# Gated linear attention and a hard-swish feed-forward block on one core: stores on another queue, idle products, and a new order

One core of a Trainium2 chip. The metric is the device time of one execution in microseconds (us), the median of several runs.

## The reference, cut to what matters

```python
# q, k, v: 4 x 8 x 768 x 48, alpha the same shape in 0.8 .. 1.0, all float32
for t in range(S):
    state = alpha[:, :, t, :, None] * state + einsum('bhd,bhe->bhde', k[:, :, t], v[:, :, t])
    y[:, :, t] = einsum('bhd,bhde->bhe', q[:, :, t], state)
x = y.transpose(0, 2, 1, 3).reshape(3072, 384)
h = x @ w_in                      # w_in 384 x 2048, float64 in memory
g = h * clip(h + 3, 0, 6) / 6
out = g @ w_out                   # w_out 2048 x 384, float64 in memory
```

## The kernel before

The sequence is cut into 24 chunks of 128 steps (index j), two chunks make a group g of 256 tokens, 12 groups in all. The kernel is one list of small steps. A step is a function that emits a few instructions; the list fixes the order on each engine. Groups 0 and 1 use plain products (`f`, `b`), while the 64-bit weights come in and are converted; the later groups use a fast matrix multiplication with fewer products (`M` for w_in, `P` for w_out).

What the argument touches:

```python
    bank_m = [ps.tile([C, GT * 2], FP, tag=f"m{i}", name=f"m{i}_ps") for i in range(4)]

    def store2(g, i):                         # 44 output stores of 96 KB
        row, col = PLACES[i]
        j = G * g + row
        nc.sync.dma_start(out=out[j * C : (j + 1) * C, col * HD : (col + 1) * HD],
                          in_=oh_t.pop((g, i)))
    # ... store(c): two more of 192 KB, also nc.sync; all loads are nc.sync too

    with tc.manual_schedule():
        run("""lk.0 la.0 lq.0 la.1 tk.0 lq.1 ta.0 ca.0 lv.1 tq.0 r.0 w.1 ta.1 ca.1 p.0 tq.1 r.1 q.0
            la.2 k.0 p.1 sc.0 lk.1 lv.0 q.1 d1.1 kb.0 m.0 w.0 d2.1 ta.2 ck.0 d3.1 tk.1 ca.2 u.0
            ...""")
```

In the list: `la lk lq lv` load chunk j, `w` loads a slice of weights and `d1`..`d4` convert it; `ta tk tq` bring alpha, k, q into the layout of the scans (`r`, `p`, on the vector engine, DVE) and `k`, `q` scale by them; `sc m kb ck u yi yx cy` are the attention products on the tensor engine (PE) with their evictions, and `cy` hands x to the first feed-forward product `f` (line L417 before, L420 after). `P` is L621 before and L630 after, `M` is L521 and L530, the outputs of DVE are L637 and L646. The scalar engine is ACT.

Of the kernel before, what the change touches and what calls it, by code (L numbers as in the profile page):

```python
# [16 lines left out]
def kernel(  # L17
# [35 lines left out]
    C = 128  # L53
# [195 lines left out]
    def load_v(j):  # L249
        to = ring["v", j % NV].rearrange("s (p a) e -> s p a e", a=2)  # L250
        sv = rows(v, j).rearrange("(p a) s d -> s p a d", a=2)
        nc.sync.dma_start(out=to[:, :, 0, 0:D], in_=sv[:, :, 0])
        nc.sync.dma_start(out=to[:, :, 1, 64 - D : 64], in_=sv[:, :, 1])
# [99 lines left out]
    def update(j):  # L353
        if last(j):
            return
        u = bank("u", j).rearrange("r p n -> r (p n)")[:, 0 : NP * 2 * D].rearrange(
            "r (p n) -> r p n", p=NP)
        ps_t["u", j] = u
        vs = ring["v", j % NV]
        for p in range(NP):  # L360

            one = vs[:, 2 * p]
            both = bass.AP(one.tensor, one.offset, [one.ap[0], (C - D, 2), (1, D)])
            nc.tensor.matmul(u[:, p], kb_t[j][:, p], both, start=True, stop=True)  # L364
# [16 lines left out]
    def within(j):  # L381
        y, A, vs = bank("y", j), A_t[j], ring["v", j % NV]
# [17 lines left out]
    def keep_x(j):  # L400
        g = j // G
        if j % G == 0:
            xT_t[g] = wk.tile([C, KT, GT], FP, tag="xT", name="xT")
# [48 lines left out]
    def store(c):  # L452
        nc.sync.dma_start(out=out[c * C : (c + 1) * C, :], in_=os_t.pop(c))
# [185 lines left out]
    def store2(g, i):  # L639
        row, col = PLACES[i]  # L640
        j = G * g + row
        nc.sync.dma_start(out=out[j * C : (j + 1) * C, col * HD : (col + 1) * HD],
                          in_=oh_t.pop((g, i)))
# [14 lines left out]
        "O": store2,  # L658
# [7 lines left out]
    with tc.manual_schedule():  # L666
        run("""lk.0 la.0 lq.0 la.1 tk.0 lq.1 ta.0 ca.0 lv.1 tq.0 r.0 w.1 ta.1 ca.1 p.0 tq.1 r.1 q.0
            la.2 k.0 p.1 sc.0 lk.1 lv.0 q.1 d1.1 kb.0 m.0 w.0 d2.1 ta.2 ck.0 d3.1 tk.1 ca.2 u.0
            k.1 d4.1 sm.0 w.4 sc.1 r.2 kb.1 ck.1 m.1 st.1 d1.0 u.1 p.2 d2.0 w.3 yi.0 d3.0 yi.1
            cy.0 yx.1 d1.4 sm.1 d4.0 d2.4 w.2 cy.1 f.0.1.0 d3.4 d1.3 st.2 d2.3 f.0.0.1 d4.4 la.3  # L670
            fr.0.1 fg.0.1 lk.2 d3.3 f.0.4.2 lv.2 fr.0.0 d1.2 lq.2 fg.0.0 d2.2 d4.3 w.5 tk.2
            fr.0.4 ta.3 d3.2 f.0.3.3 ca.3 r.3 lk.3 tq.2 fr.0.3 k.2 d4.2 w.6 q.2 fg.0.4 sc.2 d1.5
            p.3 d2.5 f.0.2.0 fg.0.3 d3.5 lq.3 tk.3 w.7 fr.0.2 kb.2 m.2 d4.5 ck.2 d1.6 k.3 u.2
            fg.0.2 d2.6 tq.3 sm.2 f.0.5.1 q.3 st.3 lv.4 d3.6 lk.5 sc.3 lv.3 fr.0.5 d1.7 fg.0.5
            la.4 yi.2 d4.6 m.3 d2.7 kb.3 w.8 yx.2 ck.3 d3.7 f.0.6.2 cy.2 d4.7 tk.5 w.9 fr.0.6
            yi.3 fg.0.6 f.0.7.3 d1.8 d2.8 lk.4 yx.3 d3.8 fr.0.7 ta.4 lq.4 cy.3 u.3 ca.4 lq.5
            d1.9 f.1.3.0 r.4 w.10 d2.9 fg.0.7 d4.8 sm.3 f.1.0.1 d3.9 fr.1.3 w.11 fg.1.3 st.4
            f.1.2.2 fr.1.0 p.4 d1.10 fg.1.0 d4.9 d2.10 tk.4 tq.4 fr.1.2 k.4 w.12 f.1.7.3 d3.10
            d1.11 fg.1.2 tq.5 d4.10 d2.11 f.1.4.0 q.4 fr.1.7 d3.11 w.13 f.1.1.1 fr.1.4 fg.1.7
            d4.11 d1.12 fg.1.4 d2.12 w.14 f.1.6.2 d3.12 fr.1.1 fg.1.1 d1.13 d4.12 b.0.0.3 d2.13  # L680
            fr.1.6 w.15 d3.13 sc.4 d1.14 fg.1.6 f.1.5.0 d4.13 m.4 d2.14 lv.5 d3.14 la.5 kb.4
            fr.1.5 yi.4 ck.4 la.6 fg.1.5 d1.15 d4.14 b.0.1 d2.15 d3.15 u.4 yx.4 sm.4 d4.15 b.0.2
            cy.4 y.1 y.5 y.6 ta.5 P.1.1.1 y.2 ca.5 x.0 r.5 b.1.0.2 y.3 p.5 b.0.3 k.5 st.5 q.5
            y.7 y.4 y.8 sc.5 bo.0 y.9 so.0 b.1.1 y.10 lq.6 m.5 y.11 la.7 y.15 yi.5 y.13 b.1.2
            y.16 y.0 tq.6 y.17 yx.5 y.12 y.19 b.1.3 cy.5 y.18 xc.2.1 y.20 xc.2.3 y.21 M.2.15.0
            xc.2.4 bo.1 s.1.0.0 P.1.0.3 s.1.1.1 x.1 s.1.4 M.2.16 K.1.0 s.1.2.2 P.1.3.2 s.1.3.3
            x.2 G.1.0 K.1.2 P.1.2 x.3 xc.2.5 y.23 M.2.0.1 xc.2.6 s.1.5 K.1.1 P.1.4 xc.2.0 xc.2.8
            xc.2.7 xc.2.2 xc.2.9 xc.2.10 y.14 ca.6 P.1.5 G.1.1 r.6 O.1.1 lq.7 y.22 P.1.6 p.6
            so.1 O.1.0 y.24 G.1.2 ca.7 M.2.7.2 n.2.0.8 tq.7 G.1.3 M.2.1 O.1.3 n.2.7.9 r.7 lk.6
            M.2.8 n.2.1.10 M.2.18.3 o.2.4.0 q.6 lk.7 e.2.4 M.2.2 p.7 n.2.18.11 M.2.17 n.2.2.12  # L690
            h.2.4 lv.6 M.2.19 tk.6 O.1.2 M.2.3 lv.7 q.7 k.6 M.2.4 la.8 tk.7 sc.6 n.2.4.13
            o.2.6.0 o.2.0.0 M.2.5 lq.8 k.7 e.2.0 M.2.9 m.6 n.2.5.14 sc.7 la.9 h.2.0 M.2.6.1
            o.2.1.0 m.7 e.2.1 M.2.10 h.2.1 kb.6 n.2.10.15 yi.6 ca.8 ck.6 M.2.11 o.2.5.0 cy.6
            tq.8 e.2.5 u.6 n.2.11.9 h.2.5 kb.7 sm.6 M.2.12 ck.7 o.2.7.0 yi.7 r.8 n.2.12.13
            M.2.13 o.2.3.0 u.7 o.2.7.1 st.7 n.2.13.12 o.2.3.1 e.2.7 M.2.14 o.2.2.0 e.2.3 yx.7
            h.2.7 h.2.3 P.2.0.3 cy.7 o.2.2.1 s.2.1.15 e.2.2 o.2.6.1 h.2.2 e.2.6 M.3.15.0
            s.2.3.11 K.2.0 h.2.6 P.2.1.1 sm.7 s.2.0.13 xc.3.1 s.2.4 M.3.16 s.2.2.12 P.2.3.2
            G.2.0 st.8 ca.9 xc.3.3 s.2.5 P.2.2 xc.3.4 K.2.2 xc.3.0 xc.3.5 r.9 xc.3.6 xc.3.7
            M.3.0.1 xc.3.8 xc.3.2 K.2.1 xc.3.9 p.8 P.2.4 n.3.0.9 xc.3.10 q.8 p.9 M.3.1 G.2.1
            O.2.1 P.2.6 n.3.1.14 lq.9 O.2.0 M.3.2 G.2.3 O.2.3 M.3.7.3 lk.8 n.3.2.10 P.2.5 tq.9  # L700
            n.3.7.8 o.3.4.0 lk.9 q.9 e.3.4 M.3.3 h.3.4 lv.8 G.2.2 M.3.8 tk.8 O.2.2 M.3.18.2 lv.9
            k.8 M.3.4 tk.9 la.10 n.3.18.13 sc.8 o.3.6.0 n.3.4.15 k.9 M.3.19 lq.10 o.3.0.0 m.8
            M.3.17 e.3.0 M.3.9 la.11 h.3.0 ca.10 sc.9 o.3.1.0 M.3.5 r.10 e.3.1 M.3.10 n.3.5.11
            h.3.1 kb.8 n.3.10.12 m.9 M.3.6.1 ck.8 M.3.11 o.3.5.0 p.10 e.3.5 u.8 n.3.11.8 yi.8
            h.3.5 sm.8 M.3.12 o.3.7.0 ca.11 st.9 yx.8 n.3.12.15 kb.9 o.3.7.1 cy.8 M.3.13 o.3.3.0
            ck.9 e.3.7 tq.10 yi.9 n.3.13.10 h.3.7 u.9 o.3.2.0 M.3.14 o.3.3.1 o.3.2.1 e.3.3 yx.9
            s.3.1.12 e.3.2 P.3.0.2 h.3.3 cy.9 h.3.2 s.3.3.13 o.3.6.1 sm.9 P.3.1.0 e.3.6 xc.4.1
            K.3.0 xc.4.0 h.3.6 xc.4.3 s.3.0.15 xc.4.4 M.4.15.1 s.3.4 P.3.3.3 s.3.2.8 G.3.0 st.10
            xc.4.5 s.3.5 P.3.2 K.3.2 xc.4.6 xc.4.7 xc.4.8 r.11 xc.4.2 M.4.0.0 xc.4.9 K.3.1
            xc.4.10 q.10 P.3.4 n.4.0.10 p.11 M.4.1 G.3.1 O.3.1 P.3.6 lq.11 n.4.1.11 O.3.0 M.4.16  # L710
            G.3.3 O.3.3 M.4.2 lk.10 M.4.7.2 tq.11 n.4.2.14 P.3.5 q.11 lk.11 n.4.7.9 o.4.4.0
            e.4.4 lv.10 h.4.4 M.4.3 tk.10 M.4.8 G.3.2 k.10 O.3.2 M.4.18.3 tk.11 lv.11 M.4.4
            n.4.18.12 la.12 k.11 sc.10 o.4.6.0 n.4.4.15 o.4.0.0 M.4.19 lq.12 m.10 e.4.0 M.4.9
            h.4.0 M.4.17 o.4.1.0 la.13 sc.11 ca.12 e.4.1 h.4.1 M.4.10 m.11 M.4.5 n.4.10.8 r.12
            kb.10 n.4.5.13 M.4.11 ck.10 o.4.5.0 M.4.6.0 n.4.11.9 p.12 e.4.5 u.10 o.4.7.0 M.4.12
            h.4.5 sm.10 yi.10 n.4.12.15 o.4.7.1 st.11 M.4.13 ca.13 e.4.7 yx.10 h.4.7 n.4.13.14
            yi.11 o.4.3.0 cy.10 o.4.2.0 M.4.14 o.4.3.1 o.4.2.1 yx.11 e.4.3 s.4.1.12 e.4.2
            P.4.0.3 h.4.3 cy.11 h.4.2 s.4.3.8 o.4.6.1 P.4.1.1 tq.12 e.4.6 K.4.0 h.4.6 xc.5.1
            s.4.0.9 xc.5.3 M.5.15.0 s.4.4 P.4.3.2 s.4.2.15 G.4.0 xc.5.4 s.4.5 xc.5.5 P.4.2
            xc.5.0 K.4.2 xc.5.6 xc.5.7 xc.5.8 r.13 xc.5.2 xc.5.9 M.5.0.1 xc.5.10 K.4.1 q.12  # L720
            P.4.4 p.13 n.5.0.14 M.5.1 G.4.1 O.4.1 P.4.6 lq.13 n.5.1.13 O.4.0 M.5.16 G.4.3 O.4.3
            M.5.2 lk.12 M.5.7.3 tq.13 n.5.2.11 P.4.5 q.13 lk.13 n.5.7.10 o.5.4.0 e.5.4 lv.12
            h.5.4 M.5.3 tk.12 M.5.8 G.4.2 k.12 O.4.2 M.5.18.2 tk.13 lv.13 M.5.4 n.5.18.9 la.14
            k.13 sc.12 o.5.6.0 n.5.4.12 o.5.0.0 M.5.19 lq.14 m.12 e.5.0 M.5.9 h.5.0 M.5.17
            o.5.1.0 la.15 sc.13 ca.14 e.5.1 h.5.1 M.5.10 m.13 M.5.5 n.5.10.8 r.14 kb.12 n.5.5.15
            M.5.11 ck.12 o.5.5.0 M.5.6.1 n.5.11.10 p.14 e.5.5 u.12 o.5.7.0 M.5.12 h.5.5 sm.12
            yi.12 n.5.12.12 o.5.7.1 st.13 M.5.13 ca.15 cy.12 e.5.7 kb.13 o.5.3.0 n.5.13.11 yi.13
            h.5.7 ck.13 o.5.2.0 M.5.14 o.5.3.1 yx.13 o.5.2.1 e.5.3 u.13 s.5.1.9 e.5.2 h.5.3
# [100 lines left out]
```

## Time and profile before

| | before |
|---|---|
| time, the 44 runs timed beside the experiments (four sets of 11, medians 585.8 to 586.4) | 584.1 to 590.2 us |
| the profiled run that the prediction read | 590.0 us (span 588.2) |
| PE busy in it | 97 % of the span |

To compare kernels I use one derived measure, **lost time**: at any matmul, the time since the start of the trace minus the sum of unit times of all useful matmuls issued before it. The unit times are those of the prediction (540.5 us for the whole kernel); idle products count as nothing. Reading the lost time at 30 us of useful work (the end of the head, about 50 to 55 us on the clock), at 200, and at the end tells in which stretch a kernel loses.

### The profile page before, as it was taken

The numbers are of one execution on the slowest core, as the hardware profiler recorded it, in microseconds if no ns is written. First come the engines' busy times: TensorE is split into PE (matmuls) and PEld (weight loads), VectorE is DVE, ScalarE is ACT, GpSimd is POOL, SyncE is SP. The second block draws the span as 40 slices with busy tenths as digits, with TensorE's granted clock in tenths as the row PEclk, the third lists the DMA queues.
The fourth block names the chain that finished last, engine by engine and source line by source line (L and its number), as shares of the span: only waits on it lengthen the run. The fifth ranks groups of instructions, "written<-read, shape, count | busy, mean of one in ns | idle before, by whom it ended". The sixth has DMA issues, their size and how long they took to land.

```text
span 588.2 us, 12191 instructions
## 1 busy us (share of the span) xinstructions
PE 568.7 (97%) x5032; PEld 527.9 (90%) x5032; DVE 474.4 (81%) x787; ACT 196.6 (33%) x335; POOL 49.7 (8%) x70
## 2 busy tenths in 40 slices
PE   5888999999999999999999999999999999999997
PEld 3777887689999899999999999999999999999997
DVE  7788698999996995995995995896897798685570
ACT  2454473012422332432331341341351251342520
POOL 2332233100000010000010010000000000000000
PEclk9598999999999999999999999999999999999999
DMA  9999754203503503503502601701700610500000
GB/s 159 212 183 195 194 158 109 64 1 104 112 1 85 119 1 77 127 3 79 123 2 53 151 1 38 161 8 34 163 7 14 161 30 1 128 1 1 2 28 27
DMA packets 87607, 45.82 MB, mean 78 GB/s; under 512 B 48896, under 2 KB 82432, under 8 KB 87552
## 3 DMA queue, kind: packets, MB, share of 16 engines
q1 hardware_dynamic: 87552, 45.05, 34.8%
q8 instruction: 39, 0.64, 0.5%
q14 instruction: 16, 0.13, 0.1%
HBM read 40.30 MB, written 4.72 MB: 77 GB/s over the span
## 4 chain that ended last, share of the span: by engine, by line
PE 71%; DVE 14%; DMA 6%; SPq 5%; issue 2%; ACT 1%; DVEq 0%; ACTq 0%
PE m_ps L621 27%; PE m_ps L521 20%; PE m_ps L417 7%; PE m_ps L443 4%; PE y_ps L386 3%; PE sc_ps L322 3%; PE u_ps L364 3%; SPq L246 2%; PE y_ps L396 2%; DMA kq<-in_k_dram 2%; DVE g_sb L425 2%; DVE g_sb L458 2%; DMA rings<-in_q_dram 2%; DVE k L268 1%; PE kb_ps L339 1%
## 5 line engine op out<-in xcount | busy, mean ns | idle before, releaser
L621 PE MATMUL m_ps<-w,g_sb 128*128 128x192 f32 x704 | 121.4, 328 | 0.2
L621 PEld LDWEIGHTS m_ps<-w,g_sb 128*128 128x128 f32 x704 | 113.7, 190 | 2.1 <-issue 0.8
L527 ACT COPY g_sb<-m_ps 128x512 f32<-128x512 f32 x110 | 64.2, 584 | 112.2 <-PE m_ps L521 110.8
L621 PE MATMUL m_ps<-rings,g_sb 128*128 128x192 f32 x528 | 91.7, 327 | 1.4 <-DVE oh L637 1.3
L521 PE MATMUL m_ps<-xc,w 128*128 128x128 f32 x640 | 86.1, 279 | 2.4 <-DVE oh L637 1.8
L621 PEld LDWEIGHTS m_ps<-rings,g_sb 128*128 128x128 f32 x528 | 85.6, 190 | 2.3 <-DVE oh L637 2.0
L521 PEld LDWEIGHTS m_ps<-xc,w 128*128 128x128 f32 x640 | 78.1, 192 | 5.4 <-DVE oh L637 2.7
L421 ACT ACTIVATE r<-g_sb,half 128x512 f32<-128x512 f32 x80 | 57.0, 721 | 75.0 <-DVE g_sb L462 34.3
L425 DVE SCALAR_TENSOR_TENSOR g_sb<-r,g_sb 128x512 f32<-128x512 f32 x80 | 54.8, 693 | 13.5 <-ACT r L421 12.1
L349 POOL TENSOR_TENSOR t<-t,R 128x384 f32<-128x384 f32 x20 | 20.0, 999 | 411.5 <-DVE t L376 229.6
L521 PE MATMUL m_ps<-xT,raw 128*128 128x128 f32 x400 | 51.6, 275 | 0.0
L521 PEld LDWEIGHTS m_ps<-xT,raw 128*128 128x128 f32 x400 | 49.4, 192 | 0.3
L268 DVE STREAM_TRANSPOSE q<-qq 128x512 f32<-128x512 f32 x18 | 20.2, 1121 | 36.5 <-DMA qq<-in_q_dram 36.5
L417 PE MATMUL m_ps<-xT,w 128*128 128x256 f32 x192 | 45.3, 392 | 1.1 <-ACT xT L404 1.1
L521 PE MATMUL m_ps<-xT,w 128*128 128x128 f32 x320 | 43.4, 279 | 0.1
L417 PEld LDWEIGHTS m_ps<-xT,w 128*128 128x128 f32 x192 | 36.9, 196 | 6.9 <-ACT xT L404 1.3
L568 DVE TENSOR_TENSOR g_sb<-g_sb 128x512 f32<-128x512 f32 (+1 forms) x55 | 41.6, 791 | 0.1
L521 PEld LDWEIGHTS m_ps<-xT,w 128*128 128x128 f32 x320 | 38.8, 192 | 1.7 <-ACT g_sb L527 0.3
L291 DVE TENSOR_TENSOR_SCAN R<-t,ones 128x516 f32<-128x516 f32 x24 | 30.1, 1252 | 4.4 <-ACT t L282 4.4
L521 PE MATMUL m_ps<-xc,raw 128*128 128x128 f32 x240 | 32.6, 279 | 0.0
L322 PE MATMUL sc_ps<-q,k 48*128 48x128 f32 x384 | 28.9, 291 | 3.5 <-DVE k L314 2.3
L521 PEld LDWEIGHTS m_ps<-xc,raw 128*128 128x128 f32 x240 | 29.7, 191 | 1.8 <-issue 1.6
(98 smaller groups left out, 711.2 us busy)
## 6 DMA issues: line engine op xcount, KB each, us to landing
raw<-in_moe_w_out_dram SPq DMA_DIRECT2D x8, 768.0 KB, 4.7
t<-in_v_dram SPq DMA_DIRECT2D x48, 96.0 KB, 2.8
raw<-in_moe_w_in_dram SPq DMA_DIRECT2D x24, 192.0 KB, 7.2
out_dram<-oh SPq DMA_DIRECT2D x44, 96.0 KB, 1.7
aq<-in_alpha_dram SPq DMA_DIRECT2D x36, 96.0 KB, 2.7
qq<-in_q_dram SPq DMA_DIRECT2D x36, 96.0 KB, 2.5
kq<-in_k_dram SPq DMA_DIRECT2D x36, 96.0 KB, 2.4
aq<-in_alpha_dram SPq DMA_DIRECT2D x36, 80.0 KB, 2.6
```

Of the source, the lines that this page charges most:

```text
L268: nc.vector.transpose(out=to.rearrange("r p (u v) -> r p v u", v=V), in_=quads[name, j % NQ][:, :, :, 0:BLK])
L291: nc.vector.tensor_tensor_scan(out=reverse(R, n - 1, n), data0=reverse(ax, n, n), data1=reverse(ones, n, n), initial=0.0, op0=ALU.mult, op ...
L322: nc.tensor.matmul(sc[h % 2][:, h // 2], K_t[j][r, h // 2], Q_t[j][r, h // 2], start=True, stop=True)
L349: nc.gpsimd.tensor_tensor(out=st[j % 2], in0=sm[j % 2], in1=R_t[j][:, :, 0:1].to_broadcast([C, NP, 2 * D]), op=ALU.mult)
L417: nc.tensor.matmul(h[:, f], w1[:, kk, o : o + C], xT_t[g][:, kk], start=(kk == 0), stop=(kk == KT - 1))
L421: nc.scalar.activation(out=to, in_=h, func=AF.Relu, bias=half, scale=1.0 / 6.0)
L425: nc.vector.scalar_tensor_tensor(out=to, in0=r, scalar=1.0, in1=h, op0=ALU.min, op1=ALU.mult)
L443: nc.tensor.matmul(o_t[c], gs[0][:, f, c * C : (c + 1) * C], w2[:, f], start=(f == 0), stop=(f == NF - 1))
L521: nc.tensor.matmul(acc[g][i][:, f * C : (f + 1) * C], spots[w][:, f * C : (f + 1) * C], x_of(g, x), start=(first and f == 0), stop=last, s ...
L527: nc.scalar.copy(out=slots[z], in_=acc[g][i])
L568: nc.vector.tensor_tensor(out=out, in0=in0, in1=in1, op=ALU.subtract)
L621: nc.tensor.matmul(to[g], a, rhs[:, f], start=(first and f == 0), stop=(last and f == HF - 1), skip_group_check=True)
```

## The change

The intent: take the output stores out of the queue in which the input loads stand, keep the tensor engine's clock up with products nobody reads, and search a new order for everything.

```diff
-    def load_v(j):
-        to = ring["v", j % NV].rearrange("s (p a) e -> s p a e", a=2)
+    def load_v(j, z):                     # the place in the ring is now named in the list
+        v_t[j] = ring["v", z]
...
     def store2(g, i):
-        nc.sync.dma_start(out=out[...], in_=oh_t.pop((g, i)))
+        nc.scalar.dma_start(out=out[...], in_=oh_t.pop((g, i)))     # store(c) likewise
...
+    def idle(m, n):
+        for _ in range(n):
+            nc.tensor.matmul(bank_m[m][:, 0:C], ones[:, 0:C], ones[:, 0:C], start=True,
+                             stop=True)
...
-        run("""lk.0 la.0 lq.0 la.1 tk.0 lq.1 ta.0 ca.0 lv.1 tq.0 r.0 w.1 ta.1 ca.1 p.0 tq.1 r.1 q.0
+        run("""z.3.6 lk.0 lq.0 la.0 la.1 tk.0 w.1 tq.0 ta.0 ca.0 ta.1 r.0 z.0.18 ca.1 lq.1 r.1 lk.1
+            p.0 w.0 d1.1 k.0 d2.1 q.0 tq.1 sc.0 p.1 tk.1 d3.1 z.0.9 lv.1.0 lv.0.1 q.1 d4.1 w.4
...                                         (the rest of the list: a new order throughout)
```

## The prediction

> **What bounds the kernel now.** I read the page first, then the windows of the first 62 us, then TensorE's timeline, the waits and the chain that ended last.
>
> ```profile
> PE 568.7 (97%) x5032; PEld 527.9 (90%) x5032; DVE 474.4 (81%) x787; ACT 196.6 (33%) x335; POOL 49.7 (8%) x70
> PEclk9598999999999999999999999999999999999999
> DMA  9999754203503503503502601701700610500000
> ```
>
> TensorE (PE) is busy for 97% of the span, so the work of other engines counts only where PE waits for it. But busy time also holds matmuls that are stretched. I therefore take, for each kind of matmul, the shortest start-to-start time that the timeline shows in a stretch without waits, and multiply by the counts of the groups table: L621 1232 x 0.1625 us (16 in 2.60) = 200.2; L521 1600 x 0.1115 (8 in 0.89) = 178.4; L417 192 x 0.215 = 41.3; L322 384 x 0.068 = 26.1; L386 768 x 0.0316 = 24.3; L443 64 x 0.322 = 20.6; L364 160 x 0.1075 = 17.2; L396 480 x 0.033 = 15.8; L339 80 x 0.110 = 8.8; L264 72 x 0.108 = 7.8. Sum 540.5 us. The profiled span is 588.2, so 47.7 us are lost: 4.1 before the first matmul, 3.3 after the last, 40.3 between.
>
> Where? At 29.78 us the first feed-forward product (L417) starts; the PE work done by then is worth 10.6 us at the units above, so 19.2 us are lost (the 4.1 included). From there to 58.75 us 23.4 us of work are done in 29.0, so 5.5 are lost. In the remaining 526.1 us, 506.5 of work, 19.6 are lost. So the first tenth holds half of the loss. Its windows (length, busy time of PE, PEld, DVE, ACT, POOL with counts, granted clock, DMA share, GB/s):
>
> ```profile
> 10.00:12.00 2.00, 0.06 (x1) 0.00 (x0) 1.97 (x4) 0.00 (x0) 0.00 (x0) 1.00 1.06 221
> 14.00:16.00 2.00, 1.61 (x8) 0.99 (x6) 1.61 (x4) 1.95 (x3) 0.00 (x0) 0.50 1.51 166
> 24.00:26.00 2.00, 2.00 (x23) 1.78 (x26) 1.44 (x3) 0.85 (x2) 0.00 (x0) 0.50 1.06 217
> 52.00:54.00 2.00, 2.00 (x6) 1.55 (x6) 1.93 (x3) 0.00 (x0) 0.00 (x0) 0.50 0.51 78
> ```
>
> The granted clock is 0.50 from about 13.3 to 26.9 us and again from 51.2 to 54.3. Two lines of PE's timeline show what that costs: sixteen score products, slow and fast.
>
> ```profile
> 19.52 2.08 PE L322 MATMUL sc_ps<-q,k 48*128 48x128 f32 x16
> 42.86 1.16 PE L322 MATMUL sc_ps<-q,k 48*128 48x128 f32 x16 [1.14 <-DVE q L314]
> ```
>
> In the body, the waits of SyncE's queue and of DVE, and the chain, show the second weakness (start, length, what):
>
> ```profile
> SPq L642 <- DVE oh L637: 313.3, 18, 47.0
> DVE q L268 <- DMA qq<-in_q_dram: 36.5, 8, 5.5
> 410.92 0.33 ACT oh L634
> 411.27 0.36 SPq L642
> 411.67 0.43 SPq L246
> ...
> 414.79 2.10 DMA kq<-in_k_dram
> ...
> 417.02 1.11 DVE k L268
> 418.13 0.20 DVE oh L637
> ...
> 418.37 1.17 PE m_ps L521 x8
> ```
>
> Output stores (L642) and input loads (L246) stand in one in-order queue. It sits 313 us behind stores whose data isn't there yet; then the loads come in a burst, DVE waits for q or k, and an output that PE needs the bank of is late. Each time PE loses little: the pieces that overran their unit time by most in the body are 1.05 us (at 180), 0.94 (281), 0.76 (463), 0.71 (198), 0.59 (417), 0.45 (549) and 0.45 (before 582), together 5.0. The other 14.6 us are excesses of 0.1 to 0.2 at nearly every change from one kind of matmul to another; they stay as long as the products are interleaved.
>
> **What the Trainium skill says.** "TensorE: Matmul & The Clock Gate", Part 1 (The HAM clock gate): the array runs at half rate by default and after an idle window, at full rate after about 3.4 us of sustained work. The trace agrees on the ratio (granted 0.50; 2.08 against 1.16 us, or 0.130 against 0.068 us start to start). Part 4 of the same page (PE-mode transpose) says that transposes do not count as busy in the same way. PE's first 6 us are only transposes, four in 1.09 us at the start and 0.60 later, which fits; it is why real products are needed to warm it. "DMA: Bandwidth & Descriptors", section Issuing engines are not separate DMA queues: a second issuing engine saves only the time of issuing. The trace adds what matters here, the wait ahead of the issue: 0.37 us to issue a store, 313 us blocked. The same TensorE page, under Engine queue depths, calls ScalarE a strict FIFO; the trace of before has no store there to show what that costs.
>
> **The change, part by part.**
>
> (1) Idle products. 40 instructions, two records each by the count of L521 (1600 records for 800 instructions): 80 x 0.1115 = 8.9 us warm, twice that cold. Six stand ahead of everything and read `ones`, which DVE finishes only at 4.3 us: 12 records x 0.223 = 2.7 us cold, so the first transpose starts at about 7.0 and not 4.14. That delays the scan chain by some 2.5 us, the first score from 12.4 to about 14.5. It should not matter, since the step after needs v. In return the clock should be full from about 8 us on. The other 34 fall into gaps; only the last (0.22 us, just ahead of the first feed-forward product) may be on the path.
>
> (2) Load order of the head. The DMA engines are saturated until about 59 us. In before, u.0 (17.60) starts when v.0 lands (17.46), behind 2.56 MB of loads. The new order has q and k of chunk 1 and weight slice w.0 ahead of v.0: 3.15 MB; at some 0.21 MB/us that is 2.8 us later, 20.3. Then at the full clock, with sc.1 already done: u.0 to 21.2, kb.1 and its copy to 22.3, u.1 to 23.2, yi.1 to 24.2, ta.2 when its alpha has landed (4.13 MB, 25.0) to 25.4, yx.1 25.8, yi.0 26.8, copy and idle product: first feed-forward product at about 27.5 against 29.78. **Gain 2.3 us.**
>
> (3) From there to 58.75. The 5.5 us lost are 1.8 of slow clock at 50.9 and gaps at 41.1, 47.1 and 48.4 (1.31, 0.84, 1.21), where q and the copy of k were late. The order puts the transposes for q a product earlier, and removing one gap keeps the clock. I take half, rounded down: **2.6 us**; the weights' conversion (DVE 17.1 of 20 us busy in 40 to 60) limits more.
>
> (4) Stores on ScalarE's queue and the order of the body. Loads of q, k and alpha are no longer behind outputs, and the new order asks for them much earlier (chunk 9's q already beside chunk 5's scan). Three of each group's seven last-stage products are moved into the next group's stretch, where DVE is nearly full (19.9 of 20 us at 380 to 400 and 420 to 440, 11.7 at 400 to 420). So most of the 5.0 us should go; **4.0 us**. Issues cost ScalarE 46 x 0.37 = 17 us, from 33% to 36% of the span: not on the path.
>
> (5) Tail. The last store's issue, 585.6, follows three others of SyncE; now it follows the copy on the same engine: **0.3 us**.
>
> Sum 2.3 + 2.6 + 4.0 + 0.3 = 9.2: 587.3 - 9.2 = 578.1, **578**.
>
> **Rivals.** (a) The head is a matter of arrival and conversion, not of clock: DMA shares above 1 in the first 50 us and the wait of u.0 on v.0 speak for it, and v.0 gets later. Then (2) and (3) give about 1 us and the time is some 582. Against: from 17.60 to 29.78 the chain is mostly PE at half rate. (b) Decoupling gives more than the visible stalls: with operands early, PE finds no late one, and part of the 14.6 us of small excesses goes too, say 5 us more, and the head gains 8 because f products follow without a stop: about 569. For it: DVE idle 36.5 us for loads. Against: windows from 60 to 180 lose almost nothing in spite of full DVE. (c) ScalarE becomes the one that blocks: it waits in order for an output of DVE before it copies the next accumulator, PE lacks a bank. A wait of 1 us once per group of eleven would cost 10 us: about 588. For it: ScalarE makes all 110 accumulator copies (L527). Against: it is idle two thirds of the time, and waits there 110.8 us for PE.
>
> **Range and chances.** Centre 578; (a) and part of (c) to 585.5, (b) to 570. Two per cent faster is under 575.6, which needs (b) in part: 0.33. Two per cent slower needs (c) far beyond its estimate: 0.02. Within: 0.65.
>
> **What would show it right or wrong.** Right: granted clock 1.00 from about 8 us through 60; the first L417 at 27 to 28 us; v.0 still the landing that u.0 waits for; SyncE's waits on outputs gone; DVE's wait for q under 10 us; in the body PE's largest overruns under 0.3 us. Wrong: a slow clock in the head all the same (idle products that don't count); L417 at 29 or later; ScalarE waiting for DVE's outputs with PE idle behind it; or a body loss that stays near 19.6 us although the loads are early.

## The result, and the profile after

The changed kernel took 581.3 us (581.0 to 582.2, four runs), before 586.9 (four runs, 585.9 to 587.9): ratio 0.9907, 95 % interval 0.9886 to 0.9928. Timed again among the experiments: 0.9922. So it is 0.8 to 0.9 % faster, some 5 us. A ratio is the mean time of one kernel's fast runs over that of the other's of the same rounds, so it is not quite the ratio of the medians quoted.

The page of the changed kernel, the lines that answer to those of before:

```profile
PE 568.0 (98%) x5112; PEld 531.3 (92%) x5112; DVE 473.4 (82%) x787; ACT 194.9 (34%) x335; POOL 53.2 (9%) x70
PEclk9999999999999999999999999999999999999999
DMA  9999797105115143440431331232242000000000
```

PE has 80 matmul records more (the idle ones), and no slice with half the clock. ACT is at 34 %; the page does not count the issuing of DMAs, and the 46 stores add 15.9 us of it. PE's timeline in the head (start us, length us, engine, line, operation, count, idle time before and what ended it):

```profile
4.25 2.93 PE L461 MATMUL m_ps<-ones 128*128 128x128 f32 x12 [4.25 <-DVE ones L114]
8.99 4.18 PE L461 MATMUL m_ps<-ones 128*128 128x128 f32 x36
20.15 1.16 PE L325 MATMUL sc_ps<-q,k 48*128 48x128 f32 x16
21.25 1.13 PE L367 MATMUL u_ps<-t,kb 128*128 128x96 f32 x8
26.73 0.63 PE L267 MATMUL ta_ps<-ident,rings 128*128 128x128 f32 x4 [1.10 <-DMA rings<-in_alpha_dram]
29.62 8.04 PE L420 MATMUL m_ps<-xT,w 128*128 128x256 f32 x36 [0.18 <-ACT xT L407]
```

The second set of sixteen scores takes 1.16 us and no longer 2.08. Yet the first feed-forward product starts at 29.62, against 29.78 in the profile of before: the head's chain did not get shorter. What stands in it is a wait of PE for alpha of chunk 2. The chain that ended last says the same (start, length, what):

```profile
14.91 2.20 SPq L172
...
18.57 8.02 DMA rings<-in_alpha_dram
...
26.73 0.63 PE ta_ps L267 x4
27.36 0.79 PE y_ps L399 x24
28.15 0.92 PE y_ps L389 x32
```

The load is issued at 18.57, behind three slices of weights (L172), and lands at 26.59. In the body, the waits of SyncE's queue (L255 loads v, L246 loads alpha, k and q) and what is left of PE's (after 60 us), each as total us, times, longest:

```profile
SPq L255 <- PE y_ps L389: 113.2, 8, 16.9
SPq L246 <- DVE q L271: 47.9, 11, 7.5
PE m_ps L630 <- DVE oh L646: 0.5, 1, 0.5
PE m_ps L630 <- DVE g_sb L467: 0.3, 2, 0.2
PE m_ps L530 <- DVE xc L467: 0.3, 1, 0.3
```

SyncE now mostly waits for buffers to come free, which costs nothing: it is ahead. DVE's wait for q is not among its dozen longest any more. Lost time, worked out from the traces as above:

| profile | first L417/L420, us | lost at 30 us of work | at 200 | at the end |
|---|---|---|---|---|
| before, as predicted from | 29.8 | 24.5 | 31.6 | 44.4 |
| before, second look | 27.1 | 22.5 | 29.7 | 40.4 |
| changed | 29.6 | 19.8 | 25.1 | 35.8 |
| changed, second look | 30.7 | 21.9 | 27.1 | 37.9 |

Two looks at one kernel differ by 2 to 4 us, and nearly all the difference arises in the head for the changed kernel, half of it for before.

### The profile page after: what moved, and what is told of

Same layout as the page of the kernel before. It is cut to its first block, busy times and chain, and to the rows that moved or that the text cites. A ratio compares the mean times of both kernels' runs of the same rounds, so it can differ in the third digit from the quotient of the medians.

```text
span 579.1 us, 12352 instructions
## 1 busy us (share of the span) xinstructions
PE 568.0 (98%) x5112; PEld 531.3 (92%) x5112; DVE 473.4 (82%) x787; ACT 194.9 (34%) x335; POOL 53.2 (9%) x70
## 4 chain that ended last, share of the span: by engine, by line
PE 90%; DVE 4%; DMA 3%; SPq 2%; issue 1%; ACT 0%; DVEq 0%
PE m_ps L630 34%; PE m_ps L530 30%; PE m_ps L420 7%; PE sc_ps L325 4%; PE m_ps L446 4%; PE y_ps L389 3%; PE y_ps L399 2%; PE u_ps L367 2%; PE kb_ps L342 1%; DMA rings<-in_alpha_dram 1%; DMA raw<-in_moe_w_in_dram 1%; SPq L172 1%; DVE g_sb L428 1%; SPq L235 1%; DVE P L305 1%
## 5 line engine op out<-in xcount | busy, mean ns | idle before, releaser
L530 PE MATMUL m_ps<-xc,w 128*128 128x128 f32 x640 | 83.0, 277 | 0.3 <-DVE xc L467 0.3
L530 PEld LDWEIGHTS m_ps<-xc,w 128*128 128x128 f32 x640 | 77.8, 192 | 2.4 <-issue 1.8
L530 PE MATMUL m_ps<-xT,raw 128*128 128x128 f32 x400 | 52.8, 279 | 0.0
L530 PEld LDWEIGHTS m_ps<-xT,raw 128*128 128x128 f32 x400 | 48.4, 192 | 1.3
L530 PE MATMUL m_ps<-xT,w 128*128 128x128 f32 x320 | 44.1, 281 | 0.0
L420 PE MATMUL m_ps<-xT,w 128*128 128x256 f32 x192 | 43.6, 382 | 0.2 <-ACT xT L407 0.2
L530 PEld LDWEIGHTS m_ps<-xT,w 128*128 128x128 f32 x320 | 38.7, 191 | 3.2 <-ACT g_sb L536 1.4
L331 DVE TENSOR_TENSOR A<-sc_ps,mask 128x512 f32<-128x512 f32 x48 | 30.8, 684 | 12.5 <-PE sc_ps L325 12.4
L420 PEld LDWEIGHTS m_ps<-xT,w 128*128 128x128 f32 x192 | 35.8, 190 | 5.6 <-issue 0.4
L530 PE MATMUL m_ps<-xc,raw 128*128 128x128 f32 x240 | 32.0, 276 | 0.0
L305 DVE TENSOR_TENSOR_SCAN P<-t 128x516 f32<-128x516 f32 x24 | 30.6, 1275 | 0.1
L467 DVE TENSOR_TENSOR g_sb<-g_sb 128x512 f32<-128x512 f32 x40 | 28.1, 703 | 2.9 <-ACT g_sb L536 2.6
```

What stands on the lines that cost most here:

```text
L305: nc.vector.tensor_tensor_scan(out=P_t[j], data0=aX[j % 2][:, 0:n], data1=ini[j % 2], initial=0.0, op0=ALU.mult, op1=ALU.add)
L331: nc.vector.tensor_tensor(out=A_t[j][:, NP * o : NP * (o + 1)], in0=ps_t.pop(("sc%d" % o, j)), in1=mask.unsqueeze(1).to_broadcast([C, NP, ...
L420: nc.tensor.matmul(h[:, f], w1[:, kk, o : o + C], xT_t[g][:, kk], start=(kk == 0), stop=(kk == KT - 1))
L467: eng.tensor_tensor(out=out, in0=in0, in1=in1, op=ALU.add if s1 > 0 else ALU.subtract)
L530: nc.tensor.matmul(acc[g][i][:, f * C : (f + 1) * C], spots[w][:, f * C : (f + 1) * C], x_of(g, x), start=(first and f == 0), stop=last, s ...
```

## The experiments

The change has three parts, so there are eight kernels with each part in or out (in the old order the idle products stand in that order's own gaps and read another tile, so there this part is not quite the same). Six experiments fill the cube beside before and the changed kernel; two look at those two again, and the rest test the head's gate and splice the two orders. All results were correct.

### Before, looked at again

No edit.

> The kernel before, unchanged, looked at a second time. Its first profile ran 590.0 us while its timed runs took 585.9 to 587.9, and its TensorE clock fell to half twice (13.3 to 26.9 us, 51.2 to 54.3 us). If the phase of the clock gate is what scatters the runs, this profile's half-clock stretches differ in place or length from the first one's and its time with them, 586 to 590 us; if the half-clock is fixed by the program, the same two stretches come back at the same places.

586.1 us, span 584.2, within the scatter of the timed runs. The half-clock is not fixed by the program:

```profile
12.48 2.08 PE L322 MATMUL sc_ps<-q,k 48*128 48x128 f32 x16 [2.35 <-DVE k L314]
19.06 1.16 PE L322 MATMUL sc_ps<-q,k 48*128 48x128 f32 x16
27.12 9.72 PE L417 MATMUL m_ps<-xT,w 128*128 128x256 f32 x36 [1.96 <-ACT xT L404]
```

Here the first scores are slow and the second fast, the reverse of the first profile, where the scores at 19.52 took 2.08 us and the first ran at nearly the full rate:

```profile
12.40 1.23 PE L322 MATMUL sc_ps<-q,k 48*128 48x128 f32 x16 [2.35 <-DVE k L314]
```

The clock falls again at 28 to 31 us, inside the first L417 (9.72 us and not 8.04), and not at 51. So the first profile was one draw of several, and a costly one: 44.4 us lost against 40.4 here.

Nor does the mean granted clock tell fast runs of before from slow ones: over its 44 timed runs it lies between 0.985 and 1.00, and the 8 runs under 0.993 took 586.7 us in the mean, the 36 others 586.3. That mean is blind to the slow clock at the very start, though (see the run without idle products), so it does not clear the clock.

### The changed kernel, looked at again

No edit.

> The changed kernel, unchanged, timed on the same chip beside the two others: ratio 0.990 to 0.992 to before. Its profile shows whether its clock is full in every run (it should be, loss at 30 us of useful work 19.5 to 21).

581.4 us (581.0 to 583.1, six runs), ratio 0.9922 (0.9904 to 0.9941). The gain holds. The profiled run was the slowest of the six (583.1), and its loss of 21.9 us in the head lies just outside the 19.5 to 21 expected; L420 starts at 30.7. After the head it loses 16.0 us, like the first look. So what these two runs differ by arises before 30 us of work: 1.0 us by alpha of chunk 2, which landed at 27.6 and not 26.6, and 1.1 by a wait for q ahead of the scores at 44.1, which the first look does not have.

### The changed kernel without idle products

```diff
-        for _ in range(n):
+        for _ in range(0):
```

> The changed kernel without its idle products (the loop runs zero times), nothing else moved. Theory (the head's gain is the clock that the idle products hold): half-clock stretches return before 60 us, the loss at 30 us of useful work rises from 19.8 us to 22 or more, and the time is 584 to 586. Rival (the head is set by arrivals and by the new order): the clock may fall, but the time stays within 1 us of 581.3, or gets better, as the first transposes start 2.7 us earlier.

584.1 us, ratio 0.9964 (0.9948 to 0.9981): 2.7 us of the gain are gone, and the theory holds. The new order's head needs the clock:

```profile
13.91 2.08 PE L325 MATMUL sc_ps<-q,k 48*128 48x128 f32 x16
18.61 2.22 PE L325 MATMUL sc_ps<-q,k 48*128 48x128 f32 x16
21.78 1.99 PE L367 MATMUL u_ps<-t,kb 128*128 128x96 f32 x8 [0.94 <-DVE w L200]
27.25 1.94 PE L389 MATMUL y_ps<-A,t 128*32 128x128 f32 x32
33.00 8.04 PE L420 MATMUL m_ps<-xT,w 128*128 128x256 f32 x36 [0.61 <-ACT xT L407]
```

Nearly everything up to 31 us runs at half rate, and L420 starts 3.4 us later. Lost at 30 us of work: 24.3, no better than before. A trap lies here: the column of the granted clock shows 1.00 in all these windows. The first clock record of this trace starts at 31.2 us; what lies before the first record is shown as 1.00, so there only the durations tell.

### The changed kernel with its stores on SyncE again

```diff
-        nc.scalar.dma_start(out=out[...], ...)
+        nc.sync.dma_start(out=out[...], ...)       # both stores
```

> The changed kernel with its 46 output stores issued from SyncE again, same order. Theory (the body's gain of 3.7 us comes from loads that no longer queue behind stores): SyncE waits for outputs again, DVE waits for q and k, TensorE has new stalls in the body, time 584 or more. Rival (the order alone takes the stalls away, the queue does not matter): within 1 us of 581.3.

582.0 us, ratio 0.9925 (0.9906 to 0.9943). The theory falls for the new order, the rival holds: SyncE does wait for outputs again, and it hurts nobody.

```profile
SPq L651 <- DVE oh L646: 110.7, 15, 29.2
...
PE m_ps L630 <- DVE oh L646: 0.5, 1, 0.5
```

From 30 us of work to the end 15.9 us are lost, as in the changed kernel (16.0).

### Before with only its stores moved

```diff
-        nc.sync.dma_start(out=out[...], ...)
+        nc.scalar.dma_start(out=out[...], ...)     # both stores, order of before
```

> The kernel before with only its output stores moved to ScalarE's queue. Theory (store queue): DVE's 36.5 us of waits for q mostly vanish and the five large stalls of the body go, 583 to 585 us. Rival (without an order that asks for the loads earlier the store's move gives nothing, or ScalarE blocks behind outputs that are not there): 586.5 or more.

582.7 us, ratio 0.9939 (0.9921 to 0.9957): two lines of code bring about two thirds of the whole gain. Here the theory holds. DVE's waits (total, times, longest) before the edit are in the prediction; after it:

```profile
DVE g_sb L460 <- ACT g_sb L527: 44.0, 9, 7.3
DVE g_sb L425 <- ACT r L421: 16.2, 18, 2.3
DVE oh L637 <- PE m_ps L621: 13.3, 8, 2.2
```

The 36 us for q are gone. In their place DVE waits 44 us for ACT's copies of accumulators. That is slack: DVE is early and waits for PE's products by way of ACT. PE's own waits after 60 us came down to 1.3 us, from 3.1 and 1.8 in the two looks at before. Lost from 30 us of work to the end: 15.0 us, against 17.9 in the second look at before. Single overruns (from one start to the next, beyond the unit time) of 0.3 us and more make up only 0.8 of these 2.9 us (2.5 before, 1.7 after); the rest are smaller ones (15.3 and 13.1 in sum).

### Before with only idle products

In the list of before: 38 idle products in eight places where the profiles showed PE waiting in the head; they read the identity, which is ready at 1.5 us.

```diff
+            nc.tensor.matmul(bank_m[m][:, 0:C], ident, ident, start=True, stop=True)
...
+ z.3.6 before lk.0, z.3.12 after tq.1, z.3.4 before u.0, z.3.2 before u.1,
+ z.3.5 before f.0.1.0, z.3.2 before f.0.3.3, z.0.4 before sc.2, z.1.3 before u.2
```

> The kernel before plus 38 idle products in the gaps of its own head, reading the identity (ready at 1.4 us, so none stands in the way of the first transpose); stores stay on SyncE. Theory (the head's gain is the full clock, no new order is needed for it): first L417 at 26 to 27 us, loss at 30 us of useful work 20 or less against 22.5 and 24.5 in the two profiles of before, time 582 to 584. Rival (the gain of the head comes from the new order): 586 or more.

585.6 us, ratio 0.9993 (0.9974 to 1.0011): nothing. The theory falls. All of PE's products after the first few run at the full rate, and what was saved is spent waiting:

```profile
12.21 1.16 PE L322 MATMUL sc_ps<-q,k 48*128 48x128 f32 x16
18.96 1.16 PE L322 MATMUL sc_ps<-q,k 48*128 48x128 f32 x16
28.37 8.04 PE L417 MATMUL m_ps<-xT,w 128*128 128x256 f32 x36 [0.92 <-ACT xT L404]
50.31 0.63 PE L264 MATMUL tq_ps<-ident,rings 128*128 128x128 f32 x4 [2.02 <-DMA rings<-in_q_dram]
```

L417 waits for the copy of x, and at 50 us PE waits 2 us for q of chunk 3, as it did at the half clock (1.77 in the second look). Lost at 30 us of work: 22.7, against 22.5. In the old order the head is set by arrivals and copies, which is rival (a) of the prediction.

### Before with stores moved and idle products

Both edits above.

> Old order, stores on ScalarE, and the same idle products: the whole change without its schedule search. If the two parts add up, 582.7 minus 2 to 4, so 579 to 580.5, at or below the changed kernel's 581.3, and the new order is worth nothing or less. If the new order matters, 582 or more.

582.0 us, ratio 0.9932 (0.9911 to 0.9952): as with the stores alone; the expected sum of the two did not come, since one of them is zero. Its six runs fall into two groups, three at 581.0 to 581.1 and three at 583.0 to 583.9. The profile is of a fast run (581.1), and in it q at 48 us was waited for 0.17 us and not 2.02. It may be that this landing makes the two groups; the slow ones were not profiled, so it stays open.

### The new order alone

Both edits of the changed kernel: no idle products, stores on SyncE.

> The new order alone: no idle products, stores on SyncE. It is the eighth corner of the cube of three parts; the other seven are measured. If the order by itself takes the steady-state stalls away, but its head without idle products is worse than the old one (loss at 30 us of useful work 24.3 in the run without idle products, against 22.5 and 24.5 before): 584 to 585, some 1.5 us less than before. If stores and order help independently of each other: 586 or more.

584.4 us, ratio 0.9966 (0.9949 to 0.9982), as expected. The cube is full:

| order | stores | idle products | median us | ratio to before | lost before the first L417/L420 | from there to 30 us of work | from there to the last matmul |
|---|---|---|---|---|---|---|---|
| old | SyncE | no | 586.4 | 1 | 19.2, 16.5 | 5.3, 6.0 | 19.9, 17.9 |
| old | SyncE | yes | 585.6 | 0.9993 | 17.8 | 4.9 | 19.1 |
| old | ACT | no | 582.7 | 0.9939 | 16.5 | 5.9 | 15.0 |
| old | ACT | yes | 582.0 | 0.9932 | 17.5 | 3.0 | 15.0 |
| new | SyncE | no | 584.4 | 0.9966 | 20.9 | 1.9 | 15.8 |
| new | SyncE | yes | 582.0 | 0.9925 | 18.9 | 2.0 | 15.9 |
| new | ACT | no | 584.1 | 0.9964 | 22.4 | 1.9 | 15.9 |
| new | ACT | yes | 581.3, 581.4 | 0.9907, 0.9922 | 19.0, 20.0 | 0.8, 1.9 | 16.0, 16.0 |

Each interval is about 0.0018 to either side; two numbers are two looks. The last three columns are lost time from the traces. The stores' queue is worth 0.6 % in the old order and 0.0 to 0.2 % in the new. The idle products are worth 0.1 % in the old order and 0.4 to 0.6 % in the new.

The columns say why. In the body, the moved stores alone and the new order alone each bring the loss to 15 or 16 us (DVE's waits for q are gone from both traces), and together they do no better: one replaces the other. Between the first feed-forward product and 30 us of work the new order gains 3 to 4 us without idle products, whichever queue the stores have, and 1 to 4 us with them. Before that product it loses more than the old order, 20.9 and 22.4 us where the clock is left to itself, and the idle products take 2 to 3 us of that back. That is why they pay in the new order and not in the old.

### Idle products that do not delay the first transposes

```diff
-            nc.tensor.matmul(bank_m[m][:, 0:C], ones[:, 0:C], ones[:, 0:C], start=True,
+            nc.tensor.matmul(bank_m[m][:, 0:C], ident, ident, start=True,
```

> The changed kernel, idle products reading the identity and not the ones, so that the first six run from 1.5 us and no longer delay the first transposes by 2.7 us. If the scan chain gates the first L417: it starts at 28 us or before and the time is 579.5. If alpha of chunk 2, which landed at 26.6 us, and the transpose that waits for it in TensorE's order gate it, as the chain of the changed kernel says: L417 stays within 0.5 us of 29.6 and the time within 0.7 us of 581.3.

582.0 us, ratio 0.9929 (0.9912 to 0.9945): no gain. The transposes start at 4.18 and not 6.97, and L420 at 29.32 (0.3 earlier):

```profile
4.18 0.75 PE L267 MATMUL tk_ps<-ident,rings 128*128 128x128 f32 x4
26.43 0.63 PE L267 MATMUL ta_ps<-ident,rings 128*128 128x128 f32 x4 [1.43 <-DMA rings<-in_alpha_dram]
29.32 8.04 PE L420 MATMUL m_ps<-xT,w 128*128 128x256 f32 x36 [0.18 <-ACT xT L407]
```

The delay is harmless, as predicted, but for another reason: alpha of chunk 2 is the gate, not v of chunk 0. Idle products do not always hold the clock: in this trace it fell once more, from 7.9 to 11.3 us, after gaps of 0.37 to 0.77 us between the transposes.

### New head, old body

The list of the changed kernel up to `f.1.3.0` (about 60 us), then the remaining steps in the old order, stores on ACT.

> The changed kernel's order up to the product f.1.3.0 (about 60 us), then the order of before, stores on ScalarE. In the profiles the loss after the first 30 us of useful work is 16.0 us in the changed kernel and 15.0 in the old order with stores on ScalarE. If that difference is real: 580 to 581, and the new body's order is not what gained. If the new body's order is needed: 582 or more.

586.0 us, ratio 0.9997. A miss, but not one about the body. Lost at 30 us of work is 19.6, as in the changed kernel; from 30 to 200 another 11.8 us go, against 5.3 there: loads that the new head would have asked for by then come in the old order's turn (PE waits 1.8 us for k in one piece). From 200 to the end it loses 8.9 us. Splicing two orders has a price at the seam.

### Old order in the steady part, first seam

The new list up to the end of group 2 (before `M.3.0.1`), then the old one, stores on ACT.

> The new order up to the end of group 2 (about 215 us), then the old order, stores on ScalarE, idle products kept. From 200 us of useful work to the end the loss is 10.5 us in the new order whatever queue the stores have, 8.6 in the old order with stores on ScalarE, 10.6 to 12.6 with them on SyncE. If this holds, the run beats both kernels: 579 to 580, some 1.9 us less than the changed kernel in the same call. If the steady part needs the new order: 581.5 or more.

586.9 us, ratio 1.0012: a miss again, by the seam. At 182 us PE stands 3.17 us for an output that DVE reaches only after the scans of two chunks; from 130 to 160 us of work 7.2 us are lost, and from 200 to the end 9.1, against 10.7 to 10.8 in the changed kernel.

### Old order in the steady part, second seam

The seam a little later (after `n.3.2.8`), so that DVE has those scans and outputs behind it; accumulator banks and slots of the old list renamed to the ones live at the seam.

> The last splice lost 7 us at its seam (DVE did the scans of chunks 8 and 9 and the x sums ahead of an output whose bank TensorE needed) and then ran with a loss of 8.9 us from 200 to 540 us of useful work, against 10.5 to 10.6 in the new order. Here the seam lies behind the outputs of group 2 and the scans of chunks 8 and 9, and accumulator banks and slots are renamed to fit. If the old order is the better one in the steady part with stores on ScalarE: loss at 200 about 25.5 to 27, end loss 34.5 to 36, time 579.5 to 580.5 and ratio 0.988 to 0.990. If the seam costs again or the old order cannot keep up without the lead it had: 582 or more.

580.2 us, ratio 0.9905 (0.9888 to 0.9923). All six runs (579.7 to 580.7) lie below all ten of the changed kernel (581.0 to 583.1), though the ratios' intervals overlap, as before ran at 585.8. Lost: 19.8 at 30, 25.1 at 200, 34.2 at the end; so 9.1 after 200, as expected from the old order. By the traces it loses least of all versions, 1.6 us less than the first look at the changed kernel; by the ratios (0.9905 against 0.9907 and 0.9922) a gain over the changed kernel is not shown. Taken apart by matmul from 200 us of work on, the new order has three gaps over 0.3 us (1.44 in all) where the old one has one (0.61), and seven more changes between kinds of products (186 against 179); a change, as from L389 to L530, costs up to 0.17 us beyond the unit time.

## Why the prediction was right or wrong

**Time: inside the range, 3.3 us above the centre** (581.3 against 578.0), and within 2 %, to which it had given 0.65. The profile that it read would have shown 9.1 us of gain in the span (588.2 to 579.1) against 9.2 predicted. That agreement is a coincidence, as the stretches show (us of lost time gained, from the traces):

| stretch | predicted | first looks | second look at before, against the two at the changed kernel |
|---|---|---|---|
| to the first feed-forward product (parts 1 and 2) | 2.3 | 0.2 | -2.5, -3.5 |
| from there to 30 us of work (part 3, reckoned to 34) | 2.6 | 4.5 | 5.2, 4.1 |
| from there to the last matmul (part 4) | 4.0 | 3.9 | 1.9, 1.9 |
| tail (part 5) | 0.3 | 0.5 | 0.5, 0.5 |
| span | 9.2 | 9.1 | 5.1, 3.1 |

**The base.** The losses were taken from a profiled run of 590.0 us and subtracted from a median of 587.3. The second look shows 4.0 us less lost (40.4), 2.0 of them in the head, where the half clock had fallen on busy stretches, and 2.0 later. The remedies were sized to losses that most runs do not have. The scatter was visible: a profiled run 2.7 us over the median.

**Part (2), the first L417 at 27.5, 2.3 us earlier: wrong.** It came at 29.6 and 30.7, which the prediction had itself named as a sign of being wrong, against 29.8 and 27.1 before. Two terms of its sum failed. One is "with sc.1 already done": v landed at 20.12, as predicted (20.3), but the second scores ran from 20.15 to 21.25, so u.0 came after them and waited for nothing. The other is "ta.2 when its alpha has landed (4.13 MB, 25.0)": alpha landed at 26.6 and 27.6, and it holds up the two products behind it in PE's order. The input queue had moved 4.75 MB by 26.59, so loads issued after alpha had already moved some 0.6 MB; a sum of the bytes issued up to alpha leaves that out. The run with the identity shows that the delay at the front did not matter. No run loads alpha earlier, so what would end this wait next is not shown.

**Part (1), the clock: right in the mechanism.** The idle products hold the full clock (recorded from 7.5 and 9.1 us on in the two looks, 8 predicted), the first transpose came at 6.97 (7.0) and the first score at 14.60 (14.5), and without idle products the new order loses 2.7 us. But it was reckoned as a gain of the clock as such. In the old order it is worth 0.4 us in the mean of runs; arrivals take its place there. Rival (a) was right about the old kernel and half right about the new one: with the clock held, a landing sets the first L420, and without idle products the half rate does (33.0). The reading that transposes do not warm the clock does not fit the profile it was read from; see the last section.

**Part (3), 2.6 us up to 58.75: right in direction, too small.** Between the first feed-forward product and 30 us of work 5.3 and 6.0 us were lost before, 0.8 and 1.9 after. Most of this is the order and not the clock: without idle products the new order loses 1.9 there as well, and the old order with idle products, at the full clock, still loses 4.9 and 3.0.

**Part (4), 4.0 us in the body: the cause right, the size too large for most runs.** From 30 us of work to the end the loss fell from 19.9 and 17.9 to 16.0 in both looks: 3.9 and 1.9. The stores in the loads' queue were the cause of this loss in the old order (2 lines give 3.6 us), and the new order cures it without that (stores back on SyncE: 0.6 us). The prediction gave its 4.0 us to the two together and did not see that either is enough. The claim that deferring three products per group to fill DVE's full stretches helps is not borne out: the old order, with stores on ACT, loses 1.6 to 1.7 us less in the steady part.

**Part (5), 0.3 us at the tail:** the time from the last matmul's end to the end of the span went from 3.3 to 2.8. The size is right, but not by the queue, which the part named: with the stores alone moved the tail stays at 3.3, and with the new order and stores on SyncE it is 2.9. The order of the last steps did it.

**Rival (c), ACT as the one that blocks:** DVE does wait more for ACT in the old order with moved stores (44.0 us against 8.6), and PE does not wait for it. Wrong, as judged.

**Rival (b)** asked for the small excesses to shrink by some 5 us. From 30 us of work on, overruns of less than 0.3 us came to 15.1 and 15.3 us in the two looks at before and 13.9 in both at the changed kernel: right in direction, a quarter of the size. At the changes of product themselves they stayed (15.5 and 15.4 before, 15.1 and 15.0 after), as the prediction said.

What stays open: why the runs of one kernel scatter by 2 us in steps, and how much of it is the landing of q and alpha in the head.

## What to carry to other kernels

Size a remedy on losses from more than one profile: here the half clock and the landings of the loads fell at other times in each look, so that the head of a single trace was a draw. When a change has several parts that could cure the same wait, test them alone and in pairs; here a two-line move of the stores gave 0.6 %, and the long search on top of it hardly more. Warming the clock gave 0.1 % where arrivals and copies ended the waits and 0.4 to 0.6 % where PE itself was late, so look at what would end the wait next before adding work that nobody reads.

## What the Trainium skill lacked or had wrong

- "DMA: Bandwidth & Descriptors", Issuing engines are not separate DMA queues: it counts only the time to initiate. That section lacks the waits ahead of an issue in an in-order queue: 313 us of SyncE's time before, and 3.6 us of 586 gained by moving 46 stores of 0.34 to 0.37 us each.
- "TensorE: Matmul & The Clock Gate", Part 4 (PE-mode transpose), on transposes not counting as busy, which the prediction followed: the first profile of before has only transposes on PE up to 10 us, its first clock record is a full one from 9.96 us, and the scores at 12.40 then took 1.23 us, while those at 19.52 took 2.08. So there transposes did release the clock. In the second look the same transposes did not: the scores at 12.48 took 2.08. What decides it is not shown.
- The same page, Part 1, has a warm-up after about 3.4 us of sustained work. It lacks how short a gap keeps a slow clock from rising: without idle products the new order ran at half rate up to 31 us, with PE busy for most of the time from 13 us on but with gaps of 0.5 to 0.9 us between. That the gaps were the cause is not shown.
- No page says that the granted clock as printed here reads 1.00 until the first clock record: sixteen scores took 2.08 us at a reading of 1.00, and the mean clock of that run is given as 1.00. (The caveats on HAM events, the trace's records of this clock, in Part 1 of the same page say to cross-check, which is what the durations do here.)
- "TensorEngine Tiling (Array Packing)", Key Properties, says that a change of tiling mode drains the engine, without a figure. Changes between kinds of small matmuls cost here 0.09 us into 32-column products or the scores, 0.17 out of the former and 0.13 out of the latter, some 15 us of this kernel after the head, which is more than all stalls that the change removed. Whether that drain is the reason is not shown.
